# Pooled attention and a rational MoE layer on one core: transfer lengths in the plan by piece size, and the softmax's remainder transposed by VectorE and placed by the weights' transfers

## The chip, the cores and the metric

The kernel runs on one core of one Trainium2 chip. The metric is device time in microseconds (us) of one execution; the result of several runs is their median. Engines are named as in the profile: PE (TensorE's matmuls), PEld (its weight loads), DVE (VectorE), ACT (ScalarE), POOL (GpSimd) and SP (SyncE, which here issues all transfers).

## The reference

```python
# q, k, v: 8 batches x 8 heads x 576 tokens x 64
k_p = k.reshape(B, H, 72, 8, D).mean(axis=3)        # keys and values pooled by 8: 72 a head
v_p = v.reshape(B, H, 72, 8, D).mean(axis=3)
scores = (q @ k_p.T) / sqrt(64)
scores = scores - max(scores)
attn = exp(scores) / (sum(exp(scores)) + 1e-09)
attn_out = attn @ v_p
# then over 4608 tokens x 512:
x = attn_out.transpose(0, 2, 1, 3).reshape(4608, 512)
h = x @ w_in                                        # 512 -> 2048
P = a0 + a1*h + a2*h**2 + a3*h**3
Q = 1 + |b0|*|h| + |b1|*h**2
out = (P / (Q + 1e-6)) @ w_out                      # 2048 -> 512
```

All is f32. The weights `w_in` and `w_out` arrive as 64-bit floats and are decoded in the kernel.

## The kernel before

The 4608 tokens go in 18 blocks of 256 (two tiles of 128 each). For a block, attention gives `x` (512 features by 256 tokens) as a rounded part and a remainder part in fp32r, so that products of three terms keep f32 accuracy. Then eight units follow, each of 256 columns of `w_in`: 24 matmuls into `ph` (`mm1`), a chain of about thirteen elementwise steps on ACT, DVE and POOL (`rational`, `quotient`), and 12 matmuls into `po` (`mm2`). Blocks 0 and 1 do their first four units, then blocks 2 and 3 theirs, while weights still arrive; blocks 4 to 17 follow one by one.

No loop order is issued as written. Every helper (`dve`, `act`, `gp`, `pe`, `dma`) adds an operation to a `Plan` with a cost in us, and `Plan.solve` simulates the engines with these costs: an operation has a due time (from `HEAD`, `SLOW` and `PACE` by the number of its unit, passed back through what it depends on, by `slack` times the cost), may not start in the plan earlier than `early` us ahead of it, and among those that can start the one due first is taken. The order so found on each engine is what is issued; on the chip each engine then keeps that order and waits where an operand is late. A transfer occupies a modelled bus for its bytes over 385 GB/s, then lands 2.2 us later; at most eight are in flight in the plan. `issue` also puts idle matmuls (`filler`, line 265 in the profile) into holes that the plan leaves on PE until 110 us.

Attention for a tile of 128 tokens (`attention`): scores `ps` (PE), maximum and difference into `e` (DVE), exponential (ACT), sum and reciprocal (DVE), normalisation (POOL). `e` holds, for each of four pairs of heads `j`, 2 x 72 = 144 weights a token. They must be transposed (pooled keys onto partitions) to be multiplied with the pooled values in `pv` (`values`). Of the 144, 128 make a full square and 16 are the remainder (`REM`).

- The 128: in blocks 0 to 3 PE transposes them (`pm`), ACT rounds them to `hi` and DVE subtracts to `lo`. From block 4 on DVE transposes 32 x 32 squares in place in `e`, and 16 transfers from `e` to `lo` (`am` in the profile) place the squares; then ACT rounds `lo` to `hi` and DVE subtracts.
- The remainder: in all blocks, ACT and DVE write a rounded and a remaining part, each twice, side by side into `er` (two casts and two subtractions a tile), PE transposes this with two `pr` transposes a tile (fp32r), and ACT copies the result to `ar`. `pv` takes `ar` as one of its four terms, with `vr` as the weights.

`q` is loaded in 32 x 32 squares too from block 4 on (`squares`). `prep_k` and `prep_v_early` or `prep_v` pool keys and values of a batch as soon as a block needs it; for the first two batches the loads go to spare weight tiles (`early`), and PE pools the values (`pvs`, `pvr`).

Of the kernel before, what the change touches and what calls it, by code (L numbers as in the profile page):

```python
# [99 lines left out]
class Plan:  # L100
# [54 lines left out]
    def solve(self):  # L155
# [15 lines left out]
        while done < len(self.ops):  # L171
# [50 lines left out]
            if op.bytes:  # L222
                bus = max(bus, op.end) + op.bytes / 385e3
                op.end = bus + 2.2
                flights = sorted(flights[1:] + [op.end])
# [61 lines left out]
def tile_pooled_attention_then_rational_moe(  # L287
# [20 lines left out]
    P = 128  # L308
# [45 lines left out]

    def dma(kbytes, dst, src, eng="sp", issue=0.48, early=60.0, after=()):
        plan.add(eng, issue, [("dma_start", (dst, src), {})], bytes=kbytes * 1024, early=early,
                 after=after)

# [57 lines left out]
    def scalars():  # L416
        dma(2, ab[:, 0:4], a.partition_broadcast(P), issue=3.7)
        dma(1, ab[:, 4:6], b.partition_broadcast(P))
        for i in range(4):
            small("tensor_scalar", out=abn[:, i:i + 1], in0=ab[:, i:i + 1],  # L420
                                scalar1=-WS ** -i, scalar2=None, op0=ALU.mult)
        act(6).activation(abn[:, 4:6], ab[:, 4:6], AF.Abs)
# [15 lines left out]
    def load_weights(kind, u):  # L438
        name = f"{kind}{u}"
        raw = new("cpool", name, [P, 2 * CW], F32, "r" + name)  # L440
        if kind == "win":
            dma(1024, raw.bitcast(I32).rearrange("p (k x) -> p k x", x=4 * P),
                w_in32[:, u * 4 * P:(u + 1) * 4 * P].rearrange("(k p) x -> p k x", p=P))
        else:
            dma(1024, raw.bitcast(I32).rearrange("p (f x) -> p f x", f=2),
                w_out32[u * 2 * P:(u + 1) * 2 * P, :].rearrange("(f p) x -> p f x", p=P))
        words = raw.bitcast(I32).rearrange("p (n t) -> p n t", t=2)
# [91 lines left out]
    def prep_v(n):  # L539
        rows = v_rows(n)  # L540
        vs_all = new("work1", "vs", [P, 512], F32, f"vs{n}")
        vs = vs_all[:, 0:NJ * D].rearrange("p (j d) -> p j d", d=D)
# [50 lines left out]
    def squares(i):  # L593
# [6 lines left out]
        for r0, r1, n in segs(i * TOK, TOK):  # L600
            s0 = i * TOK + r0 - n * S
            for j in range(NJ):
                for g in range(4):
                    hh, d0 = g // 2, g % 2 * HB
                    dma(3 * (r1 - r0) // 8, qs[g * HB:(g + 1) * HB, j, r0 // HB:r1 // HB, :],
                        q[n, 2 * j + hh, s0:s0 + r1 - r0, d0:d0 + HB].rearrange(
                            "(b s) d -> s b d", s=HB))
        return qs

    def attention(t, am, ar, qs, es):  # L610

# [7 lines left out]
        else:  # L619
# [3 lines left out]
            for r0, r1, n in sg:  # L623
                s0 = t * P + r0 - n * S
                dma(512, qt[r0:r1], q[n, :, s0:s0 + (r1 - r0), :].rearrange("h s d -> s h d"))
            pq = bank(f"pq{t}", [P, NJ, P])
# [4 lines left out]
            act(NJ * P).copy(qT, pq)  # L631
        e = es[:, :, t % 2].rearrange("p j (h s) -> p j h s", s=SP)
        mx = new("work2", "mx", [P, H], F32, f"mx{t}")
        sm = new("work2", "sm", [P, H], F32, f"sm{t}")
        for c in range(2):
# [6 lines left out]
                for jj in range(2) for r0, r1, n in sg], claims=(e, mx, sm))  # L642
# [5 lines left out]
                    [P, 2, 2, SP]), op=ALU.subtract)  # L648
        ef = es[:, :, t % 2]
        act(H * SP).activation(ef, ef, AF.Exp, scale=D ** -0.5)  # L650
# [14 lines left out]
        hi, lo = am  # L665
        if t >= 8:
            squares = ef[:, :, REM:].rearrange("p j (g s) -> p j g s", s=HB)
            dve(NJ * P).transpose(squares, squares)
        else:
            pm = bank(f"pm{t}", [P, NJ, P])  # L670
            pe(109 * NJ, [("transpose", (pm[:, j, :], ef[:, j, REM:], ident), {})
                          for j in range(NJ)], claims=am)
            act(NJ * P).copy(hi[:, :, col], pm)
            dve(NJ * P).tensor_tensor(
                out=lo[:, :, col], in0=pm, in1=hi[:, :, col].bitcast(F32), op=ALU.subtract)
# [5 lines left out]
    def values(i, am, ar):  # L681

        hi, lo = am
# [24 lines left out]
    def attend(i):  # L708

        for _, _, n in segs(i * TOK, TOK):  # L710
            if n not in prepared:
                prepared.add(n)
                prep_k(n)
                (prep_v_early if n < 2 else prep_v)(n)
        am = [new("work1", f"am{s}", [P, NJ, TOK], F32R, f"am{s}_{i}") for s in range(2)]
        ar = new("work1", "ar", [P, 2, TOK], F32R, f"ar{i}")
        qs = squares(i)
        es = new("work1", "e", [P, NJ, 2, 2 * SP], F32, f"e{i}")
        for m in range(2):
            attention(2 * i + m, am, ar, qs, es)  # L720
        if i >= 4:

            hi, lo = am
# [6 lines left out]
            hi, lo = (x.rearrange("p j t -> p (j t)") for x in am)  # L730
            act(NJ * TOK).copy(hi, lo.bitcast(F32))
            dve(NJ * TOK, port=True).tensor_tensor(
                out=lo, in0=lo.bitcast(F32), in1=hi.bitcast(F32), op=ALU.subtract)
        return values(i, am, ar)


    def spill(i, xs):
        kept = []
        for s, x in enumerate(xs):
            d = new("hbm", f"xd{s}_{i}", [P, NJ, TOK], F32, f"xd{s}_{i}")  # L740
            dma(512, d, x.bitcast(F32))
            kept.append(d)
        return kept

    def reload(i, kept):
        xs = [new("work2", f"x{s}", [P, NJ, TOK], F32R, f"xr{s}_{i}") for s in range(2)]
        for x, d in zip(xs, kept):
            dma(512, x.bitcast(F32), d)
        return xs
# [180 lines left out]
```

## Time and profile before

| | |
|---|---|
| median of 3 runs | 962.45 us (959.35 to 963.65) |
| profiled execution | 965.26 us |
| its span | 963.6 us, granted clock 0.993 |
| matmuls on PE | 6261 |
| transfers `am<-e` | 224 of 32 KB |
| moved by DMA | 71.65 MB, 156692 packets |

The span is the time from the first to the last instruction of the profiled execution. A row of a group of instructions gives its line, engine, operation, the tiles written and read, their shapes and the count; then its busy time in us and the mean duration of one in ns; then how long the engine stood idle just ahead of such instructions and what ended that. Since operations are recorded by one helper, nearly all have line 268 (265 for the idle matmuls), so the tiles' names tell them apart. Matmuls are pipelined: what one costs is read from start to start, not from its duration.

### The profile page before, as it was taken

The page shows a single profiled execution, that of the slowest core. Times are in us where ns is not written, and L with a number is a line of the kernel's source. Part 1 is how long each engine was busy: PE and PEld are TensorE (multiplying, and loading weights), DVE is VectorE, ACT ScalarE, POOL GpSimd, SP SyncE. Part 2 cuts the span into 40 slices and gives each one's busy share as a digit, 9 for nine tenths or more (in the row PEclk, how much of TensorE's full clock was granted, in tenths as well). Part 3 has the DMA queues.
Part 4 walks back from the last instruction along what each step waited for, and adds up shares of the span by engine and source line. Part 5 has one row for each costly group of instructions (what it writes and reads, how often), then busy time and mean ns, then how long its engine had stood idle before and what let it go on. Part 6 is the DMA issues. An engine that isn't in the chain of part 4 may idle for free.

```text
span 963.6 us, 17331 instructions
## 1 busy us (share of the span) xinstructions
PE 948.0 (98%) x6261; PEld 860.5 (89%) x6261; DVE 781.6 (81%) x1346; ACT 694.5 (72%) x1180; POOL 509.1 (53%) x445
## 2 busy tenths in 40 slices
PE   8899999999999999999999999999999999999998
PEld 7888899988998999999999899989999899999996
DVE  6787988888888978798888897979787988787664
ACT  4676888958676767676777686776867686767674
POOL 4465556847455645445745374547544654544343
PEclk9989999999999999999999999999999999999999
DMA  9965210154133213122313240214211411102000
GB/s 305 336 233 182 70 57 1 44 138 125 48 70 72 66 20 92 17 51 61 107 18 63 56 122 7 36 41 121 52 28 46 93 41 27 41 1 45 1 22 22
DMA packets 156692, 71.65 MB, mean 74 GB/s; under 512 B 133952, under 2 KB 133952, under 8 KB 156608
## 3 DMA queue, kind: packets, MB, share of 16 engines
q1 hardware_dynamic: 156608, 70.56, 28.0%
q8 instruction: 49, 0.80, 0.3%
q14 instruction: 35, 0.29, 0.1%
HBM read 50.60 MB, written 12.58 MB: 66 GB/s over the span
## 4 chain that ended last, share of the span: by engine, by line
PE 88%; DVE 4%; DMA 2%; SPq 2%; ACT 2%; issue 1%; DVEq 0%
PE po L268 39%; PE ph L268 39%; PE pv L268 4%; PE ps L268 3%; SPq L268 2%; DVE t L268 2%; DMA early<-in_v_dram 2%; DMA q<-in_q_dram 1%; DVE m_wout L268 1%; PE pr L268 1%; PE pk L265 0%; DVE rp L268 0%; ACT t L268 0%; PE pk L268 0%; PE ph L265 0%
## 5 line engine op out<-in xcount | busy, mean ns | idle before, releaser
L268 PEld LDWEIGHTS ph<-x,win 128*128 128x128 f32 x3264 | 482.3, 188 | 61.1 <-ACT t L268 0.8
L268 PE MATMUL ph<-x,win 128*128 128x256 f32 x3264 | 500.8, 281 | 0.6 <-ACT t L268 0.4
L268 PE MATMUL po<-wout,gh 128*128 128x512 f32 x1152 | 358.5, 397 | 0.0
L268 POOL TENSOR_TENSOR w<-w,r 128x512 f32<-128x512 f32 (+1 forms) x145 | 189.7, 1308 | 263.5 <-ACT r L268 252.6
L268 POOL TENSOR_TENSOR gl<-t,gh 128x512 fp32r<-128x512 f32 (+1 forms) x145 | 192.6, 1328 | 100.6 <-ACT gh L268 100.3
L268 PEld LDWEIGHTS po<-wout,gh 128*128 128x128 f32 x1152 | 182.3, 189 | 7.3 <-ACT gh L268 0.2
L268 PE MATMUL po<-wout,gl 128*128 128x512 f32 x576 | 181.6, 396 | 0.0
L268 DVE TENSOR_TENSOR t<-t,ph 128x512 f32<-128x512 f32 (+1 forms) x145 | 97.9, 675 | 61.9 <-ACT t L268 60.1
L268 DVE SCALAR_TENSOR_TENSOR t<-t,abn,rp 128x512 f32<-128x512 f32 (+1 forms) x145 | 106.9, 737 | 48.9 <-ACT rp L268 46.2
L268 ACT ACTIVATE w<-ph 128x512 f32<-128x512 f32 (+1 forms) x145 | 86.1, 594 | 73.6 <-PE ph L268 68.1
L268 ACT ACTIVATE rp<-w,cbias 128x512 f32<-128x512 f32 (+1 forms) x145 | 99.9, 689 | 43.7 <-POOL w L268 41.2
L268 ACT ACTIVATE r<-w,abn 128x512 f32<-128x512 f32 (+1 forms) x145 | 117.9, 813 | 10.7 <-POOL gl L268 4.4
L268 ACT ACTIVATE t<-ph,abn 128x512 f32<-128x512 f32 (+1 forms) x145 | 110.8, 765 | 20.2 <-PE ph L268 14.4
L268 DVE SCALAR_TENSOR_TENSOR t<-t,abn,ph 128x512 f32<-128x512 f32 (+1 forms) x145 | 107.5, 742 | 6.3 <-ACT w L268 1.3
L268 ACT CAST gh<-t 128x512 fp32r<-128x512 f32 (+1 forms) x145 | 88.3, 609 | 23.0 <-DVE t L268 19.9
L268 DVE SCALAR_TENSOR_TENSOR t<-rp,t 128x512 f32<-128x512 f32 (+1 forms) x145 | 99.3, 685 | 4.3
L268 DVE SCALAR_TENSOR_TENSOR rp<-w,rp 128x512 f32<-128x512 f32 (+1 forms) x145 | 99.1, 683 | 0.2
L268 PEld LDWEIGHTS po<-wout,gl 128*128 128x128 f32 x576 | 91.1, 189 | 4.1 <-issue 0.6
L268 ACT ACTIVATE rp<-rp 128x512 f32<-128x512 f32 (+1 forms) x145 | 84.0, 579 | 3.4 <-DVE t L268 0.5
L268 POOL TENSOR_TENSOR e<-e,sm 128x576 f32<-128x576 f32 x36 | 41.5, 1159 | 30.8 <-DVE sm L268 22.3
L268 POOL TENSOR_TENSOR st_v<-st_v 128x512 f32<-128x512 f32 (+1 forms) x36 | 36.5, 1018 | 38.1 <-DMA st_v<-in_v_dram 12.1
L268 PE MATMUL pv<-am,vm 128*128 128x256 f32 (+3 forms) x288 | 47.9, 286 | 0.5 <-DVE kpT L268 0.4
(95 smaller groups left out, 870.3 us busy)
## 6 DMA issues: line engine op xcount, KB each, us to landing
out_dram<-ob SPq DMA_DIRECT2D x17, 512.0 KB, 3.1
rwin<-in_moe_w_in_dram SPq DMA_DIRECT2D x8, 1024.0 KB, 9.0
rwout<-in_moe_w_out_dram SPq DMA_DIRECT2D x8, 1024.0 KB, 10.3
am<-e SPq DMA_DIRECT2D x224, 32.0 KB, 2.0
st_k<-in_k_dram SPq DMA_DIRECT2D x12, 512.0 KB, 4.5
st_v<-in_v_dram SPq DMA_DIRECT2D x12, 512.0 KB, 3.9
q<-in_q_dram SPq DMA_DIRECT2D x144, 32.0 KB, 2.0
st_v<-in_v_dram SPq DMA_DIRECT2D x48, 64.0 KB, 3.8
```

The source lines that it names most:

```text
L268: getattr(engines[op.eng], name)(*map(value, args), **{k: value(v) for k, v in kw.items()})
```

## The change

In the plan: a transfer's bytes are counted as `kbytes * (1 + 312 / run)`, with `run` the length in bytes of its contiguous pieces, over 390 instead of 385 GB/s; the `kbytes` of several transfers are set to their true size in exchange. `HEAD`, `PACE` and one `slack` change, and the `issue` cost of the scalars' load.

In the computation: `e` gets two more columns of squares (`NJ + 2`), and so does `lo`, in place of `er` and `ar`. In blocks 4 to 17 DVE transposes the 2 x 16 remainders of two pairs of heads into each of them, four times side by side; the 16 transfers that place the squares carry these two along (six squares a piece of work instead of four). After the landing ACT rounds the lower 64 partitions of these columns in place, writes the rounded upper 64 to a part of `e`, and DVE subtracts that from the upper 64. In blocks 0 to 3 ACT copies the four-fold remainder (f32), PE transposes it (f32, two a tile), ACT copies the result to `lo` rounded, and DVE subtracts on the upper 64 partitions.

```diff
-                bus = max(bus, op.end) + op.bytes / 385e3
+                bus = max(bus, op.end) + op.bytes / 390e3
...
-    def dma(kbytes, dst, src, eng="sp", issue=0.48, early=60.0, after=()):
-        plan.add(eng, issue, [("dma_start", (dst, src), {})], bytes=kbytes * 1024, early=early,
-                 after=after)
+    def dma(kbytes, dst, src, run=2048, issue=0.48, early=60.0, after=()):
+        plan.add("sp", issue, [("dma_start", (dst, src), {})], early=early, after=after,
+                 bytes=kbytes * 1024 * (1 + 312 / run))
...
-        dma(2, ab[:, 0:4], a.partition_broadcast(P), issue=3.7)
+        dma(2, ab[:, 0:4], a.partition_broadcast(P))
...  # load_weights "wout", spill, reload: run=4096
-        vs_all = new("work1", "vs", [P, 512], F32, f"vs{n}")
+        vs_all = new("work1", "vs", [P, (NJ + 2) * D], F32, f"vs{n}")
...  # squares(i), the q loads of blocks 4 to 17
-                    dma(3 * (r1 - r0) // 8, qs[g * HB:(g + 1) * HB, j, r0 // HB:r1 // HB, :],
+                    dma((r1 - r0) / 8, qs[g * HB:(g + 1) * HB, j, r0 // HB:r1 // HB, :],
...                         run=128
...  # attention, the q loads of blocks 0 to 3
-                dma(512, qt[r0:r1], q[n, :, s0:s0 + (r1 - r0), :].rearrange("h s d -> s h d"))
+                dma(2 * (r1 - r0), qt[r0:r1],
+                    q[n, :, s0:s0 + (r1 - r0), :].rearrange("h s d -> s h d"), run=256)
...
-        er = new("work2", "er", [P, 2, 2, 2, 2, REM], F32R, f"er{t}")
-        rem = ef[:, :, 0:REM].rearrange("p (c m) r -> p c m r", m=2)
-        for c in range(2):
-            esrc = rem[:, c].unsqueeze(1).to_broadcast([P, 2, 2, REM])
-            act(90).copy(er[:, c, 0], esrc)
-            dve(60, port=True).tensor_tensor(
-                out=er[:, c, 1], in0=esrc, in1=er[:, c, 0].bitcast(F32), op=ALU.subtract)
+        main = pairs[:, 0:NJ, REM:]
+        rem = [pairs[:, 2 * c:2 * c + 2, 0:REM].unsqueeze(1).to_broadcast([P, 4, 2, REM])
+               for c in range(2)]
+        four = [pairs[:, NJ + c, REM:].rearrange("p (g m r) -> p g m r", g=4, m=2)
+                for c in range(2)]
         if t >= 8:
+            for c in range(2):
+                dve(P).transpose(four[c], rem[c])
+            squares = main.rearrange("p j (g s) -> p j g s", s=HB)
             dve(NJ * P).transpose(squares, squares)
         else:
...
+            for c in range(2):
+                act(P).copy(four[c], rem[c])
+            pr = bank(f"pr{t}", [P, 2, P])
+            pe(109 * 2, [("transpose", (pr[:, c, :], pairs[:, NJ + c, REM:], ident), {})
+                         for c in range(2)])
+            act(2 * P).copy(lo[:, NJ:, col], pr)
+            dve(2 * P).tensor_tensor(
+                out=lo[P // 2:, NJ:, col], in0=pr[P // 2:],
+                in1=lo[P // 2:, NJ:, col].bitcast(F32), op=ALU.subtract)
-        pr = new("ps", "ps", [P, 2, P], F32R, f"pr{t}")
-        pe(63 * 2, [("transpose", (pr[:, c, :], er[:, c].rearrange("p a g m r -> p (a g m r)"),
-                                   identr), {}) for c in range(2)], claims=(ar,))
-        act(2 * P).copy(ar[:, :, col], pr.bitcast(F32))
...  # values
-                             (pv[:D, jj, r0:r1], vr[n % 2][:, j, :], ar[:, c, r0:r1]),
+                             (pv[:D, jj, r0:r1], vr[n % 2][:, j, :], lo[:, NJ + c, r0:r1]),
...  # attend
-        am = [new("work1", f"am{s}", [P, NJ, TOK], F32R, f"am{s}_{i}") for s in range(2)]
-        ar = new("work1", "ar", [P, 2, TOK], F32R, f"ar{i}")
+        hi, lo = (new("work1", f"am{s}", [P, NJ + 2 * s, TOK], F32R, f"am{s}_{i}")
+                  for s in range(2))
...
-        es = new("work1", "e", [P, NJ, 2, 2 * SP], F32, f"e{i}")
+        es = new("work1", "e", [P, NJ + 2, 2, 2 * SP], F32, f"e{i}")
...
-                    dma(96, lo[g * HB:(g + 1) * HB].rearrange(
+                    dma(48, lo[g * HB:(g + 1) * HB].rearrange(
                         "p j (m a s) -> p j m a s", m=2, s=HB)[:, :, :, a, :].bitcast(F32),
-                        es[a * HB:(a + 1) * HB, :, :, k0:k0 + HB], issue=0.65)
+                        es[a * HB:(a + 1) * HB, :, :, k0:k0 + HB],
+                        run=128, issue=0.65)
...
+            half = slice(P // 2, P)
+            act(2 * TOK).copy(lo[0:P // 2, NJ:], whole[0:P // 2, NJ:])
+            own = es[half, 0:2, :, 0:P]
+            both = [x[half, NJ:].rearrange("p c (m s) -> p c m s", m=2) for x in (lo, whole)]
+            act(2 * TOK).copy(own.bitcast(F32R), both[1])
+            dve(2 * TOK, port=True).tensor_tensor(
+                out=both[0], in0=both[1], in1=own, op=ALU.subtract)
...
-    HEAD, PACE, SLOW, SLOWS = 31.0, 6.3, 5.0, 2 * NA
+    HEAD, PACE, SLOW, SLOWS = 25.0, 6.1, 5.0, 2 * NA
...
-            plan.slack = 1.6
+            plan.slack = 1.4
             xs[i, again] = reload(i, kept.pop(i)) if again else attend(i)
```

More of the change, by code (lines that the diff above doesn't have):

```diff
@@ L445, in load_weights @@
             dma(1024, raw.bitcast(I32).rearrange("p (f x) -> p f x", f=2),
-                w_out32[u * 2 * P:(u + 1) * 2 * P, :].rearrange("(f p) x -> p f x", p=P))
+                w_out32[u * 2 * P:(u + 1) * 2 * P, :].rearrange("(f p) x -> p f x", p=P), run=4096)
         words = raw.bitcast(I32).rearrange("p (n t) -> p n t", t=2)
@@ L604, in squares, with attention @@
                     hh, d0 = g // 2, g % 2 * HB
-                    dma(3 * (r1 - r0) // 8, qs[g * HB:(g + 1) * HB, j, r0 // HB:r1 // HB, :],
+                    dma((r1 - r0) / 8, qs[g * HB:(g + 1) * HB, j, r0 // HB:r1 // HB, :],
                         q[n, 2 * j + hh, s0:s0 + r1 - r0, d0:d0 + HB].rearrange(
-                            "(b s) d -> s b d", s=HB))
+                            "(b s) d -> s b d", s=HB), run=128)
         return qs
-    def attention(t, am, ar, qs, es):
+    def attention(t, hi, lo, qs, es):
         sg = segs(t * P, P)
@@ L631, in attention @@
             act(NJ * P).copy(qT, pq)
-        e = es[:, :, t % 2].rearrange("p j (h s) -> p j h s", s=SP)
+        pairs = es[:, :, t % 2]
+        e = es[:, 0:NJ, t % 2].rearrange("p j (h s) -> p j h s", s=SP)
         mx = new("work2", "mx", [P, H], F32, f"mx{t}")
@@ L648, in attention @@
                     [P, 2, 2, SP]), op=ALU.subtract)
-        ef = es[:, :, t % 2]
+        ef = es[:, 0:NJ, t % 2]
         act(H * SP).activation(ef, ef, AF.Exp, scale=D ** -0.5)
@@ L657, in attention @@
                 [P, NJ, 2, SP]), op=ALU.mult)
-        er = new("work2", "er", [P, 2, 2, 2, 2, REM], F32R, f"er{t}")
-        rem = ef[:, :, 0:REM].rearrange("p (c m) r -> p c m r", m=2)
-        for c in range(2):
-            esrc = rem[:, c].unsqueeze(1).to_broadcast([P, 2, 2, REM])
-            act(90).copy(er[:, c, 0], esrc)
-            dve(60, port=True).tensor_tensor(
-                out=er[:, c, 1], in0=esrc, in1=er[:, c, 0].bitcast(F32), op=ALU.subtract)
-        hi, lo = am
+        main = pairs[:, 0:NJ, REM:]
[3 more added lines that the diff above has]
+                for c in range(2)]
         if t >= 8:
-            squares = ef[:, :, REM:].rearrange("p j (g s) -> p j g s", s=HB)
+            for c in range(2):
+                dve(P).transpose(four[c], rem[c])
+            squares = main.rearrange("p j (g s) -> p j g s", s=HB)
             dve(NJ * P).transpose(squares, squares)
@@ L670, in attention, with values @@
             pm = bank(f"pm{t}", [P, NJ, P])
-            pe(109 * NJ, [("transpose", (pm[:, j, :], ef[:, j, REM:], ident), {})
-                          for j in range(NJ)], claims=am)
+            pe(109 * NJ, [("transpose", (pm[:, j, :], main[:, j], ident), {})
+                          for j in range(NJ)], claims=(hi, lo))
             act(NJ * P).copy(hi[:, :, col], pm)
             dve(NJ * P).tensor_tensor(
-                out=lo[:, :, col], in0=pm, in1=hi[:, :, col].bitcast(F32), op=ALU.subtract)
-        pr = new("ps", "ps", [P, 2, P], F32R, f"pr{t}")
-        pe(63 * 2, [("transpose", (pr[:, c, :], er[:, c].rearrange("p a g m r -> p (a g m r)"),
-                                   identr), {}) for c in range(2)], claims=(ar,))
-        act(2 * P).copy(ar[:, :, col], pr.bitcast(F32))
-    def values(i, am, ar):
-        hi, lo = am
+                out=lo[:, 0:NJ, col], in0=pm, in1=hi[:, :, col].bitcast(F32), op=ALU.subtract)
+            for c in range(2):
[7 more added lines that the diff above has]
+                in1=lo[P // 2:, NJ:, col].bitcast(F32), op=ALU.subtract)
+    def values(i, hi, lo):
         xs = [new("work2", f"x{s}", [P, NJ, TOK], F32R, f"x{s}_{i}") for s in range(2)]
@@ L714, in attend @@
                 (prep_v_early if n < 2 else prep_v)(n)
-        am = [new("work1", f"am{s}", [P, NJ, TOK], F32R, f"am{s}_{i}") for s in range(2)]
-        ar = new("work1", "ar", [P, 2, TOK], F32R, f"ar{i}")
+        hi, lo = (new("work1", f"am{s}", [P, NJ + 2 * s, TOK], F32R, f"am{s}_{i}")
+                  for s in range(2))
         qs = squares(i)
-        es = new("work1", "e", [P, NJ, 2, 2 * SP], F32, f"e{i}")
+        es = new("work1", "e", [P, NJ + 2, 2, 2 * SP], F32, f"e{i}")
         for m in range(2):
-            attention(2 * i + m, am, ar, qs, es)
+            attention(2 * i + m, hi, lo, qs, es)
         if i >= 4:
-            hi, lo = am
             for a in range(4):
@@ L726, in attend @@
                     k0 = REM + g * HB
-                    dma(96, lo[g * HB:(g + 1) * HB].rearrange(
+                    dma(48, lo[g * HB:(g + 1) * HB].rearrange(
                         "p j (m a s) -> p j m a s", m=2, s=HB)[:, :, :, a, :].bitcast(F32),
-                        es[a * HB:(a + 1) * HB, :, :, k0:k0 + HB], issue=0.65)
-            hi, lo = (x.rearrange("p j t -> p (j t)") for x in am)
-            act(NJ * TOK).copy(hi, lo.bitcast(F32))
+                        es[a * HB:(a + 1) * HB, :, :, k0:k0 + HB],
+                        run=128, issue=0.65)
+            whole = lo.bitcast(F32)
+            act(NJ * TOK).copy(hi, whole[:, 0:NJ])
             dve(NJ * TOK, port=True).tensor_tensor(
-                out=lo, in0=lo.bitcast(F32), in1=hi.bitcast(F32), op=ALU.subtract)
-        return values(i, am, ar)
+                out=lo[:, 0:NJ], in0=whole[:, 0:NJ], in1=hi.bitcast(F32), op=ALU.subtract)
+            half = slice(P // 2, P)
[5 more added lines that the diff above has]
+                out=both[0], in0=both[1], in1=own, op=ALU.subtract)
+        return values(i, hi, lo)
     def spill(i, xs):
@@ L740, in spill @@
             d = new("hbm", f"xd{s}_{i}", [P, NJ, TOK], F32, f"xd{s}_{i}")
-            dma(512, d, x.bitcast(F32))
+            dma(512, d, x.bitcast(F32), run=4096)
             kept.append(d)
@@ L747, in reload @@
         for x, d in zip(xs, kept):
-            dma(512, x.bitcast(F32), d)
+            dma(512, x.bitcast(F32), d, run=4096)
         return xs
```

## The prediction

> **What bounds the kernel now.** I read the busy lines of the page first, then the busy time by stretches, then what PE waited for.
>
> ```profile
> PE 948.0 (98%) x6261; PEld 860.5 (89%) x6261; DVE 781.6 (81%) x1346; ACT 694.5 (72%) x1180; POOL 509.1 (53%) x445
> 24.10:60.00 35.90, 33.19 (x238) 31.71 (x237) 25.23 (x45) 24.75 (x43) 16.54 (x10) 0.90 1.00 334
> 40.00:50.00 10.00, 8.15 (x43) 7.24 (x43) 5.36 (x10) 3.98 (x9) 2.16 (x2) 0.79 1.06 334
> 50.00:60.00 10.00, 10.00 (x71) 9.75 (x70) 7.69 (x10) 7.74 (x13) 5.24 (x4) 0.86 0.94 320
> 60.00:80.00 20.00, 18.07 (x119) 17.42 (x118) 14.40 (x24) 12.77 (x20) 10.92 (x7) 0.83 0.38 138
> 500.00:600.00 100.00, 100.00 (x673) 90.86 (x672) 85.26 (x148) 73.11 (x126) 52.89 (x45) 1.00 0.26 60
> ```
>
> A row by stretches gives the length, then PE, PEld, DVE, ACT and POOL busy, the granted clock, the DMA share and GB/s. There are two regimes. From about 106 us on, PE has no holes (100.00 of 100, clock 1.00); the other engines and the DMA have room, and only fewer PE microseconds shorten the time. Before that the head is bound elsewhere: DMA share 1.00 at 334 GB/s until 60 us, and the granted clock falls to 0.79 to 0.86 between 40 and 80. What PE waited for from 106 us to the end are five waits that sum to 2.0 us, of which this is the longest:
>
> ```profile
> PE pk L268 <- DVE ks L268: 0.6, 1, 0.6
> ```
>
> **The change, part by part.** The profiled execution took 965.26 us, its span 963.6; the median of the runs is 962.45, 2.8 lower. I make the sum against 965.26 and carry the difference over to the median.
>
> *Transposes of the remainder leave PE, blocks 4 to 17.* Each of these 14 blocks has four `pr` transposes (two tiles, two each). PE's timeline with and without them, at the same mix of neighbours:
>
> ```profile
> 543.85 0.63 PE L268 MATMUL ph<-x,win 128*128 128x256 f32 x4
> 544.32 0.46 PE L268 MATMUL pr<-identr,er 128*128 128x128 f32 x4
> 544.62 0.70 PE L268 MATMUL po<-wout,gh 128*128 128x512 f32 x2
> 545.15 0.63 PE L268 MATMUL ph<-x,win 128*128 128x256 f32 x4
> ...
> 504.43 0.64 PE L268 MATMUL ph<-x,win 128*128 128x256 f32 x4
> 504.90 0.62 PE L268 MATMUL po<-wout,gh 128*128 128x512 f32 x2
> 505.36 0.63 PE L268 MATMUL ph<-x,win 128*128 128x256 f32 x4
> L268 PE MATMUL pr<-identr,er 128*128 128x128 f32 x72 | 9.2, 242 | 1.5 <-DVE t L268 0.9 <-ACT ar L268 0.5 <-DVE er L268 0.2
> ```
>
> From `ph` to `ph` it is 1.30 us with them and 0.93 without: 0.37 us a block, 14 times, 5.2 us. Ends: start to start alone, 0.30 x 14 = 4.2; the group's busy time, 9.2 x 56/72 = 7.2. I take 5.2, since it includes what the neighbours lose. It is all on the path, since PE is never idle there.
>
> *Blocks 0 to 3* keep two transposes per tile, now f32 instead of fp32r. The nearest f32 transposes are `pm`:
>
> ```profile
> 95.11 0.60 PE L268 MATMUL pm<-identr,e 128*128 128x128 f32 x4
> 95.47 0.70 PE L268 MATMUL po<-wout,gl 128*128 128x512 f32 x2
> ```
>
> Four in 0.36 us, 0.09 each, as the `pr` above (0.37/4). I take 0; the ends are -0.3 and +0.3 us for 16. The DVE subtraction now follows `pr` instead of going ahead of it; the chain has as many steps as before.
>
> *ACT, DVE and POOL, blocks 4 to 17.*
>
> ```profile
> L268 ACT CAST er<-e 128x64 fp32r<-128x64 f32 x72 | 13.8, 240 | 9.4 <-POOL e L268 8.9
> L268 ACT CAST ar<-pr 128x256 fp32r<-128x256 f32 x36 | 11.9, 376 | 2.4 <-PE pr L268 2.3
> L268 DVE TENSOR_TENSOR er<-e,er 128x64 fp32r<-128x64 f32 x72 | 21.1, 336 | 0.5 <-ACT er L268 0.5
> L268 ACT CAST x<-pv 128x512 fp32r<-128x512 f32 x36 | 21.1, 586 | 19.5 <-PE pv L268 19.4
> L268 DVE TENSOR_TENSOR x<-pv,x 128x512 fp32r<-128x512 f32 x36 | 24.5, 686 | 15.0 <-ACT x L268 14.9
> L268 DVE STREAM_TRANSPOSE e<-e 128x512 f32<-128x512 f32 x28 | 18.6, 689 | 0.0
> L268 ACT CAST am<-am 128x1024 fp32r<-128x1024 f32 x14 | 14.6, 1042 | 5.8 <-DMA q<-in_q_dram 4.7 <-DMA am<-e 1.1
> ```
>
> ACT loses four casts `er` and two `ar` a block (0.96 + 0.75 = 1.71 us) and gains two 512-element copies on 64 partitions (0.59 each by `x`, 1.18): 0.5 us less. DVE loses four subtractions (0.29 each, 21.1/72: 1.17) and gains four 128-element transposes and one 512-element subtraction (0.69). A transpose of 512 takes 0.69; I estimate 0.30 for 128, between a quarter of that and the 0.34 of the 64-element row, so 1.89 in all: 0.7 us more a block. DVE is at 85% in these stretches, so 43 becomes 44 of 50 us; its cover is the 7 us a block in which it is idle. POOL does nothing new. Cost 0 on the path, end +0.
>
> *The transfers that place the weights* stay 16 a block and 128 bytes a piece, but grow from 32 to 48 KB each.
>
> ```profile
> am<-e SPq DMA_DIRECT2D x224, 32.0 KB, 2.0
> q<-in_q_dram SPq DMA_DIRECT2D x144, 32.0 KB, 2.0
> q<-in_q_dram SPq DMA_DIRECT2D x48, 8.0 KB, 1.6
> L268 SPq DMA_DIRECT2D am<-e x224: 585/609/1797, 225.1 to 877.9; - x112
> ```
>
> From 8 to 32 KB landing grows by 0.4 us, so 16 KB more cost about 0.3 us. Issue takes SP 0.61 us; between no growth and growth with the pieces (0.91) I take the lower, since nothing shows growth, and keep 4.9 us a block as the end. Queued behind them on SP are the next block's `q` loads and the output's store. The Trainium skill ("DMA: Bandwidth & Descriptors", "Why small descriptors are slow (HBM only)") says that transfers inside SBUF do not pay for small pieces as those from HBM do; the two 32 KB rows above, one from SBUF and one from HBM, both land in 2.0 us, so here the latency hides any such difference.
>
> *The new tail of the chain, and who waits for it.* After the last landing stood one ACT cast and one DVE subtraction; now two ACT copies (1.18) and a DVE subtraction (0.69) follow before `pv` has its third operand, and two transposes (0.6) stand ahead of the transfers: with the landing 1.18 + 0.69 + 0.6 + 0.3 = 2.8 us. On PE, `pv` has all later `ph` and `po` behind it. The tightest of the 14 blocks and the next tightest (the last row is for the sentence behind):
>
> ```profile
> 492.75 1.22 DVE L268 TENSOR_TENSOR am<-am,am 128x1024 fp32r<-128x1024 f32 x1
> 496.70 0.39 PE L268 MATMUL pv<-am,vm 128*128 128x256 f32 x2
> ...
> 291.19 1.22 DVE L268 TENSOR_TENSOR am<-am,am 128x1024 fp32r<-128x1024 f32 x1
> 298.51 0.47 PE L268 MATMUL pv<-am,vm 128*128 128x256 f32 x2 [0.44 <-DVE kpT L268]
> ...
> 500.00 1.14 PE L268 MATMUL ps<-kpT,qT 128*128 128x144 f32 x8
> ```
>
> 2.7 us lie between in the first pair, 6.1 in the second, more in the other twelve. So 0 to 0.1 us there, and 0 elsewhere. `e` serves as scratch in the tail and is held some 3 us longer; the next block writes it after its first `ps`, at 500.00, 6.0 us behind the end of the subtraction in the tightest block, which covers that.
>
> *The plan.* `issue` for the scalars' load falls from 3.7 to 0.48 us, which moves what SP does next that much forward in the plan alone. A full 1 MB transfer was planned at 2.72 us (1 MiB over 385 GB/s); now 3.10 in 2 KB runs. At the 334 GB/s of the stretch from 24 to 60 us it takes 3.14. So the plan comes to know that loads land later. What this is worth lies in the head:
>
> ```profile
> 41.91 1.10 PE L268 MATMUL pvs<-early,identr 128*128 128x256 f32 x4
> 44.87 2.82 PE L268 MATMUL pvr<-early,fourfold 32*128 32x128 f32 x16 [1.85 <-DMA early<-in_v_dram]
> 69.31 4.76 PE L265 MATMUL pk<-identr 128*128 128x128 f32 x23 [1.93 <-DVE t L268]
> 74.17 3.70 PE L265 MATMUL ph<-identr 128*128 128x256 f32 x20
> ```
>
> PE was sent to `pvr` before its transfer had landed, stood 1.9 us, and lost clock: (1 - 0.79) x 10 + (1 - 0.86) x 10 = 3.5 us. That hole costs 5.4. A plan with true landing times puts ready `ph` work there. I take half, 2.7, since an order that is filled in one place can open in another; ends -5.4 (gone) and +5.4 (a second such hole). The second hole, 69 to 78, waits on DVE and is filled by 8.5 us of idle matmuls; I leave it, with 1.9 + 8.5 = 10.4 us as the far end. The Trainium skill ("TensorE: Matmul & The Clock Gate", Part 1) puts the loss of clock behind an idle window of about 3.4 us; here 1.9 us of waiting, after thin work, was enough, so I price by the rows.
>
> *HEAD, PACE, slack.* `HEAD` 31 to 25 and `PACE` 6.3 to 6.1 bring due times forward, attention's slack 1.6 to 1.4 puts its chain later against the weights; the head's idle matmuls may end 6 us sooner. After 106 us there are only 2.0 us of waits to win, so 0; in the head it is part of the -5.4 to +5.4.
>
> Sum: 965.26 - 5.2 - 2.7 = 957.4 against the profiled execution, 954.6 against the median.
>
> **The rivals.**
> - Only the transposes count; the head's holes move but stay: 962.45 - 5.2 = 957.3. For it: DMA share 1.00 until 60 us, whatever the order.
> - Both holes of the head go: 962.45 - 5.2 - 5.4 - 10.4 = 941.5 at most, some 946 if half of the second one goes. Against it: that one is DVE's backlog, and DVE gets no less to do.
> - The new order opens a second hole like that at 44.87 (fillers end sooner, weights go ahead of `v`): 962.45 - 5.2 + 5.4 = 962.7, no change. By the page of the Trainium skill named above a hole below 3.4 us would cost its wait alone, 1.9 instead of 5.4, so 959.2; the 0.79 of the clock row here speaks against it.
> - Slower: the longer tail reaches `pv` in blocks 4 to 17. If smaller slack in the plan brings the margins of 6 us and more down to nothing, each block waits up to 2.8 us, 39 in all; at half of that 954.6 + 20 = 974. It decides from 0.9 us a block on ((967.3 - 954.6)/14). For it: the margin of 2.7 us in one block. Against it: the other margins.
>
> **How the numbers follow.** Forecast 0.40 (its own range 950 to 957.6), only the transposes 0.20, both holes 0.15, a new hole 0.15, late `pv` 0.10. Within 0.5% means 957.6 to 967.3, about what a measurement of this kernel tells from no change. Faster: 0.40 + 0.11 of the second case, which sits on the bound, + 0.15 = 0.66. Same: 0.09 + 0.12 + 0.02 = 0.23. Slower: 0.03 + 0.08 = 0.11. The range, 945 to 963, leaves out late `pv` and the best of both holes.
>
> **What would show it.** In the profile after: `pr` 16 instead of 72 on PE and 0.93 us between neighbours in blocks 4 to 17; `am` transfers of 48 KB landing in about 2.3 us; DVE's share in the stretches from 200 on up one to two points with PE still at 100; no wait of PE `pvr` on a load and a clock above 0.9 from 40 to 60. Wrong if PE waits for `pv`'s operands after 200 us, if a 128-element transpose takes far over 0.30, or if the head, up to the point where PE runs without holes, is later than before.

## The result, and the profile after

The changed kernel takes 955.11 us (median of 5 runs, 954.91 to 955.53) against 960.92 of the kernel before beside it (5 runs, 959.35 to 963.65): ratio 0.9936, 95% interval 0.9917 to 0.9955. It is faster by 0.64%, forecast at 954.6. Together with the runs beside the experiments it is 955.0 (11 runs, 953.38 to 955.76) against 962.3 (the 91 runs of the kernel before beside the experiments, 957.88 to 970.07), 7.3 us less. The two profiled executions, 965.26 and 955.0, lie 10.3 us apart; part of that is chance in the kernel before, as e3 shows.

The page's busy line and clock line, then rows by stretches (length, PE, PEld, DVE, ACT and POOL busy, granted clock, DMA share, GB/s):

```profile
PE 938.6 (98%) x6203; PEld 851.1 (89%) x6203; DVE 801.7 (84%) x1352; ACT 693.7 (73%) x1124; POOL 509.9 (53%) x445
...
PEclk9989999999999999999999999999999999999999
```

```profile
40.00:50.00 10.00, 10.00 (x86) 9.96 (x85) 9.37 (x12) 10.00 (x16) 8.27 (x5) 1.00 1.07 329
50.00:60.00 10.00, 8.53 (x45) 7.23 (x44) 9.74 (x16) 5.34 (x9) 5.01 (x3) 0.89 1.03 377
60.00:80.00 20.00, 18.57 (x108) 15.37 (x108) 14.74 (x23) 15.22 (x25) 11.71 (x9) 0.88 0.36 129
...
500.00:600.00 100.00, 99.90 (x666) 90.38 (x665) 90.42 (x153) 73.15 (x118) 54.80 (x45) 1.00 0.31 65
```

PE is busy 9.4 us less, and is still nearly without holes once the head is over (0.1 us in this stretch, 2.3 in the 824 from 106 to 930). DVE is busy 20 us more: at 90 of 100 in this stretch where it had 85. The stretch from 40 to 50, at clock 0.79 before, is full now. Where the profile before lost clock from 40 to 60 and once more from 60 to 80 (0.83), this one loses it from 50 to 80 alone.

The groups that took the place of `er`, `ar` and 56 of the 72 `pr` (busy us, mean ns of one, idle ahead of it):

```profile
L268 PE MATMUL pr<-identr,e 128*128 128x128 f32 x16 | 3.1, 277 | 0.0
L268 DVE STREAM_TRANSPOSE e<-e 128x128 f32<-128x128 f32 x56 | 14.2, 280 | 3.8 <-POOL e L268 3.7
L268 DVE TENSOR_TENSOR am<-am,e 64x512 fp32r<-64x512 f32 x14 | 9.8, 698 | 0.4
L268 ACT CAST e<-am 64x512 fp32r<-64x512 f32 x14 | 8.7, 618 | 0.3
am<-e SPq DMA_DIRECT2D x224, 48.0 KB, 2.2
L268 SPq DMA_DIRECT2D am<-e x224: 585/618/1821, 217.6 to 870.6; - x112
```

What PE waited for in the head and after it, the longest rows:

```profile
PE pk L268 <- DVE ks L268: 2.0, 2, 1.6
PE idle L268 <- DVE identr L909: 1.7, 1, 1.7
PE pvr L268 <- DVE t L268: 1.5, 1, 1.5
PE ps L268 <- ACT qT L268: 1.1, 1, 1.1
PE pm L265 <- DVE am L268: 1.1, 1, 1.1
PE ph L265 <- DVE e L268: 0.9, 1, 0.9
```

No row of the whole list names a transfer, and none names `pv`. The chain's new tail in the tightest of the 14 blocks, between DVE's last subtraction and `pv`:

```profile
288.50 0.69 DVE L268 TENSOR_TENSOR am<-am,e 64x512 fp32r<-64x512 f32 x1
...
291.14 0.40 PE L268 MATMUL pv<-am,vm 128*128 128x256 f32 x2
```

It ends 1.95 us ahead of it (288.50 + 0.69 to 291.14); in the second profile of the same kernel (e5) the same block has 1.63.

### The profile page after: what moved, and what is told of

It reads as the page before. It is cut to its first block, busy times and chain, and to the rows that moved or that the text cites. A ratio compares the mean times of both kernels' runs of the same rounds, so it can differ in the third digit from the quotient of the medians.

```text
span 953.3 us, 17151 instructions
## 1 busy us (share of the span) xinstructions
PE 938.6 (98%) x6203; PEld 851.1 (89%) x6203; DVE 801.7 (84%) x1352; ACT 693.7 (73%) x1124; POOL 509.9 (53%) x445
## 4 chain that ended last, share of the span: by engine, by line
PE 81%; DVE 6%; ACT 4%; SPq 3%; issue 2%; POOL 2%; DMA 1%; DVEq 0%; POOLq 0%; ACTq 0%
PE ph L268 36%; PE po L268 35%; PE ps L268 4%; PE pv L268 3%; SPq L268 3%; DVE t L268 2%; ACT rp L268 1%; PE idle L265 1%; PE pvs L268 1%; DMA am<-e 1%; POOL w L268 1%; DVE m_win L268 1%; POOL gl L268 1%; DVE rp L268 1%; DVE e L268 1%
## 5 line engine op out<-in xcount | busy, mean ns | idle before, releaser
L268 ACT ACTIVATE e<-e 128x576 f32<-128x576 f32 x36 | 24.3, 681 | 40.8 <-DVE e L268 40.8
```

The costliest lines, as they stand in the source:

```text
L268: getattr(engines[op.eng], name)(*map(value, args), **{k: value(v) for k, v in kw.items()})
```

## The experiments

Times are medians. Comparisons of less than 1% are made at equal granted clock too, for the reason that e3 gives; times at a given clock are means over the runs with that mean clock.

**e3: the kernel before, again.** No edit.

> The kernel before, unchanged, for a second profile. The runs so far lie between 959.35 and 965.26, those of after within 0.6 us. Theory: the spread of before arises in the head, where PE waits for a load at about 45 us and loses clock: the start of block 4's pv lies some us earlier than the 251.3 of the first profile, and from there to the end it takes the same 712 us within 0.5. Rival: the spread is spread over the whole run, in proportion.

Measured: 962.53 (959.37 to 967.54, 12 runs). Its profile is one of the better executions, 960.81 us with span 959.1. The same stretches as in the prediction's first fence:

```profile
40.00:50.00 10.00, 8.70 (x49) 7.90 (x50) 5.57 (x8) 3.74 (x7) 3.30 (x2) 0.84 1.07 339
50.00:60.00 10.00, 10.00 (x82) 9.81 (x81) 8.90 (x11) 9.30 (x15) 5.72 (x5) 0.99 1.03 359
60.00:80.00 20.00, 18.10 (x131) 16.02 (x129) 16.11 (x32) 14.84 (x24) 11.09 (x8) 1.00 0.40 143
```

The same program, the same two waits on the `early` load (2.0 and 1.0 us here, 0.9 and 1.9 in the first profile), and yet a clock of 0.99 and 1.00 where it was 0.86 and 0.83. In narrower stretches the clock stands at 0.50: for 6.8 us, twice, in the first profile, and for 3.4 us, once, in this one. One such row of each:

```profile
45.90:52.70 6.80, 6.80 (x31) 6.49 (x31) 1.34 (x3) 3.16 (x6) 2.39 (x1) 0.50 0.91 320
46.70:50.10 3.40, 3.40 (x18) 3.40 (x18) 0.69 (x1) 1.77 (x3) 2.14 (x1) 0.50 1.02 393
```

That is 6.8 and 1.7 us of PE's time lost (half of 13.6 and of 3.4). Where the two executions part is seen at the first `pv` rows of block 4 (instructions' shortest/mean/longest in ns, then the stretch in us), the first profile and then this one:

```profile
L268 PE MATMUL pv<-am,vm x24: 271/275/317, 251.3 to 254.4; 128*128 128x128 f32 x24
```

```profile
L268 PE MATMUL pv<-am,vm x24: 271/275/318, 246.3 to 249.4; 128*128 128x128 f32 x24
```

5.0 us lie between them there, for 5.1 us of lost clock; from there to the end of the span it is 712.3 us (963.6 - 251.3) and 712.8 (959.1 - 246.3). So between these two executions of one kernel the difference arises in the head, in the clock that its thin stretches lose in one execution and keep in another. The 91 runs of the kernel before, by their mean granted clock (80 of them; the other 11 lie between these columns or below 0.989):

| granted clock | 1.000 | 0.998 | 0.996 | 0.995 | 0.993 | 0.991 | 0.989 |
|---|---|---|---|---|---|---|---|
| mean, us | 958.6 | 960.2 | 962.2 | 963.6 | 965.4 | 966.8 | 969.0 |
| runs | 7 | 23 | 14 | 8 | 16 | 9 | 3 |

About 1 us for each 0.001 of mean clock, which is what 0.001 of a span of 960 us comes to. The runs are from three chips, whose means at 0.998 are 960.0, 960.2 and 960.3. The Trainium skill ("TensorE: Matmul & The Clock Gate", Part 1) says that the window in which the gate counts busy cycles runs freely, so that the moment of a change of clock varies from run to run; that fits this table, and the stretches of 3.4 and 6.8 us at 0.50; no run here shows what the gate counts. Against this, the changed kernel's 11 runs split into 955.1 at 0.996 (6) and 954.4 at 0.998 (5). At equal clock the change is worth 7.1 us (0.996) and 5.8 us (0.998). The changed kernel pays 0.7 us for the same 0.002 that cost the kernel before 2.0, so this comparison too depends on the clock at which it is made.

**e1: the new computation alone, with the plan of before** (the lengths of before, its `issue` of 3.7, HEAD, PACE and slack).

```diff
-                bus = max(bus, op.end) + op.bytes / 390e3
+                bus = max(bus, op.end) + op.bytes / 385e3
...
-                 bytes=kbytes * 1024 * (1 + 312 / run))
+                 bytes=kbytes * 1024)
...
-    HEAD, PACE, SLOW, SLOWS = 25.0, 6.1, 5.0, 2 * NA
+    HEAD, PACE, SLOW, SLOWS = 31.0, 6.3, 5.0, 2 * NA
...
-            plan.slack = 1.4
+            plan.slack = 1.6
```

> The new computation (remainder transposed by VectorE from block 4 on, carried by the weights' transfers) under the plan of before: 385 GB/s without the term for the pieces, HEAD 31, PACE 6.3, slack 1.6, issue 3.7. Theory: taking the pr transposes off PE is worth 4 to 5 us by itself: about 956.0 (0.995 of before), and PE's waits after 106 us stay under 4 us. Rival: the new order of the plan carries the gain and the transposes give nothing net, since DVE and the longer tail take it back: 960 to 962.

**e2: the old computation with the new plan**, the same edits the other way, in the kernel before.

> The computation of before (pr on PE, er, ar) under the new plan: lengths by pieces, 390 GB/s, HEAD 25, PACE 6.1, slack 1.4, issue 0.48. Theory: 1 to 2 us faster than before, from the head alone: 959 to 960. Rival (the plan carries the gain): 955 to 956. A second rival (the new due times suit only the new computation): 962 to 966.

Measured: e1 955.57 us (954.05 to 960.08, 9 runs), ratio 0.9933, interval 0.9906 to 0.9960: the whole gain without the plan. e2 963.87 (962.01 to 966.11, 12 runs), ratio 1.0020, 0.9997 to 1.0042: nothing, or 1 to 2 us lost. At equal clock (0.996) e1 takes 954.6 and the changed kernel 955.1; e2 takes 964.2 at 0.993 and 962.8 at 0.995, about 1 us less than the kernel before there (965.4 and 963.6), but none of its runs lies above 0.995. So the plan's new numbers bring nothing that shows in the time, with either computation. The stretches that lose most in e1, and in e2, and in e2 the longest wait there:

```profile
60.00:80.00 20.00, 15.89 (x92) 13.50 (x91) 16.35 (x32) 11.15 (x18) 9.27 (x7) 0.83 0.70 231
```

```profile
80.00:106.00 26.00, 20.89 (x94) 15.18 (x95) 21.43 (x39) 16.79 (x30) 13.27 (x9) 0.80 0.35 110
94.81 0.73 PE L268 MATMUL po<-wout,gh 128*128 128x512 f32 x2 [2.14 <-ACT gh L268]
```

In e1 the stretch 40 to 60 is full at clock 1.00, with no wait on the load, although its plan has the old, too short times of the loads; it loses from 60 to 80 instead. In e2 that stretch has clock 1.00, and most of the loss is at 80 to 106. Each order has its thin place in the head, somewhere else in each. e1 loses clock once more in the middle: 3.4 us at half clock from 537 on, behind a wait of 1.8 us on DVE. Lost clock is not confined to the head.

**e4: two f32 transposes a tile back on PE in blocks 4 to 17.** Their results go to a bank that nobody reads.

```diff
                 dve(P).transpose(four[c], rem[c])
+            pr = bank(f"pr{t}", [P, 2, P])
+            pe(109 * 2, [("transpose", (pr[:, c, :], main[:, c], ident), {}) for c in range(2)])
             squares = main.rearrange("p j (g s) -> p j g s", s=HB)
             dve(NJ * P).transpose(squares, squares)
```

> After, with two f32 transposes a tile on PE put back in blocks 4 to 17 (of the weights' first two squares, into a bank that nothing reads): extra work, so that only PE's price of them is measured. Theory: PE has no holes there, so all 56 show, 0.09 each: 955.1 + 5.0 = 960.1 (4.2 to 5.2 more). Rival: PE has slack there that hides them: 955 to 956.

Measured: 962.77 us (957.34 to 964.86, 12 runs), at equal clock 962.3 (0.998) and 964.2 (0.996), so 8 to 9 us more than the changed kernel, and more than the 5.0 expected. It does not price the transposes alone: PE reads `e` here, which DVE transposes in place, so DVE has to wait for PE. But in the profiled execution, the fastest of the twelve (957.34, clock 1.00), that happens once:

```profile
DVE e L268 <- PE pr L268: 0.7, 1, 0.7
```

So this wait is not shown to be the cause of the excess, which stays open. e6 does without it.

**e6: the same transposes, of the identity**, which wait for nothing and which nobody waits for; and **e5: the changed kernel again**, beside it.

```diff
+            pr = bank(f"pr{t}", [P, 2, P])
+            pe(109 * 2, [("transpose", (pr[:, c, :], ident, ident), {}) for c in range(2)])
```

> After, with two f32 transposes of the identity a tile on PE in blocks 4 to 17, which wait for nothing and which nothing reads: PE's price of 56 transposes by itself, without the wait that the earlier version of this put between PE and VectorE's transposes. Compared at equal granted clock with after. Theory: 0.09 each, 5.0 more (4.2 to 5.8). Rival: the whole 7 us by which after is lower at equal clock is PE's price: 7 or more.

> After, unchanged, among runs of before on one chip. In the runs so far the time goes with the granted clock of the whole run: before took 958 at 1.000, 960 at 0.998, 962 at 0.996, 965 at 0.993, 967 at 0.991. Theory: that is the clock PE loses in the head, another amount in each execution; after follows the same line about 7 us lower: 955 at 0.996, 951 to 952 at 1.000 if that comes, 958 at 0.993. Rival: after is steadier than before and stays within 1 us.

Measured: e5 954.5 us (953.38 to 955.76, 6 runs), ratio 0.9903, 0.9873 to 0.9933: 955.1 at 0.996 as the theory had it, but 954.2 at 0.998, where its line gives 953, and a spread of 2.4 us, so neither the theory nor the rival holds. e6 960.76 (958.19 to 962.2, 12 runs), ratio 0.9969, 0.9948 to 0.9990. At equal clock that is 6.2 us (0.998) and 6.5 us (0.996) above the changed kernel, for 56 transposes on PE and the order that the planner makes with them: between the theory's 4.2 to 5.8 and the rival's 7. In PE's timeline of e6 (start, duration):

```profile
402.94 0.63 PE L268 MATMUL ph<-x,win 128*128 128x256 f32 x4
403.40 0.62 PE L268 MATMUL po<-wout,gh 128*128 128x512 f32 x2
403.87 0.60 PE L268 MATMUL pr<-identr 128*128 128x128 f32 x4
404.22 0.72 PE L268 MATMUL ph<-x,win 128*128 128x256 f32 x4
404.77 0.63 PE L268 MATMUL po<-wout,gl 128*128 128x512 f32 x2
```

Four take 0.35 us from start to start (403.87 to 404.22), and the `ph` behind them 0.55 to the next start where it takes 0.46 without (402.94 to 403.40): 0.43 to 0.44 us a block, 6.1 in 14. That agrees with the time of the whole: once the head is over, more work on PE shows as time.

**e7: blocks 0 to 3 as before**, with the fp32r remainder `er` from ACT and DVE ahead of PE (in the buffer of `ks`, since its own is gone).

```diff
-            for c in range(2):
-                act(P).copy(four[c], rem[c])
-            pr = bank(f"pr{t}", [P, 2, P])
...
+            er = new("work1", "ks", [P, 2, 2, 2, 2, REM], F32R, f"er{t}")
+            for c in range(2):
+                esrc = old[:, c].unsqueeze(1).to_broadcast([P, 2, 2, REM])
+                act(90).copy(er[:, c, 0], esrc)
+                dve(60, port=True).tensor_tensor(
+                    out=er[:, c, 1], in0=esrc, in1=er[:, c, 0].bitcast(F32), op=ALU.subtract)
...
+            act(2 * P).copy(lo[:, NJ:, col], pr.bitcast(F32))
```

> After, with the remainder in blocks 0 to 3 formed as before (two casts and two subtractions a tile into a tile er, which shares its place with ks, two fp32r transposes on PE, one copy). Compared at equal clock with after. Theory: of the 7 us at equal clock 2 to 3 come from the head, by the new form in blocks 0 to 3: 957 to 958 at 0.996. Rival: the form in the head is worth nothing (955 to 955.5 at 0.996), and blocks 4 to 17 carry all.

Measured: 957.01 us (955.28 to 958.18, 7 runs), ratio 0.9931, 0.9902 to 0.9960; at equal clock 956.2 (0.998) and 957.5 (0.996), so 1.8 to 2.4 us more than the changed kernel, from three runs at each clock (at 0.998 two lie near 955.3 and one at 957.8). Its thin place lies late in the head:

```profile
80.00:106.00 26.00, 21.78 (x137) 18.55 (x136) 20.45 (x45) 17.35 (x32) 10.96 (x8) 0.87 0.45 144
```

Whether these 2 us are the old form's own work, its buffers, or the other order that the planner makes around it, this run doesn't tell: the order of the head differs from the first blocks on, and the table further down shows that its profile loses them behind block 4's start.

**e8: DVE's new 128-element transposes done twice**, 56 more of them.

```diff
-                dve(P).transpose(four[c], rem[c])
+                for _ in range(2):
+                    dve(P).transpose(four[c], rem[c])
```

> After, with the 56 transposes of the remainder on VectorE in blocks 4 to 17 done twice (the second repeats the first): 14 us more on VectorE in all, 1.0 a block, its share from 88 to 90% in the middle. Theory: still off the path, since pv's operands are ready 2 us and more ahead: 955 to 957 at 0.996. Rival: VectorE is at its limit, and PE waits for most of it: 962 to 969.

Measured: 955.7 us (953.92 to 958.37, 6 runs), ratio 0.9916, 0.9884 to 0.9947; at clock 0.998 955.1 (three runs, 953.9 to 955.8), 0.7 us more than the changed kernel. The group, and six blocks in the middle, first of e8 and then, for the same stretch, of the changed kernel:

```profile
L268 DVE STREAM_TRANSPOSE e<-e 128x128 f32<-128x128 f32 x112 | 28.7, 290 | 6.0 <-POOL e L268 4.3
200.00:500.00 300.00, 297.86 (x1960) 269.73 (x1959) 264.02 (x474) 218.69 (x354) 164.43 (x136) 1.00 0.33 71
```

```profile
200.00:500.00 300.00, 299.81 (x1983) 272.43 (x1982) 263.61 (x459) 218.66 (x356) 160.85 (x136) 1.00 0.33 73
```

The transposes take 14.5 us more (28.7 by 14.2), and the time grows by 0.7 us, as the theory had it. But DVE as a whole is busy only 6.6 us more (808.3 by 801.7), and in the 300 us shown only 0.4, since other operations of DVE came out shorter. PE has 2.1 us of holes in the 300 instead of 0.2.

**e9 and e10: the plan's two halves undone one at a time**, in the changed kernel: e9 the due times (HEAD 31, PACE 6.3, slack 1.6, with the new lengths), e10 the lengths and `issue` (with the new due times). The edits are the two halves of e1's.

> After with HEAD 31, PACE 6.3 and slack 1.6 as before; the lengths by pieces stay. The plan as a whole gave nothing at equal clock (after 955.1 at 0.996, the new computation under the old plan 954.6), but after's runs lie within 2.4 us (953.4 to 955.8), those under the old plan within 6 (954.1 to 960.1). Theory: the lengths by pieces are what steadies the head, so this one stays within 2.5 us and at 954 to 956.5. Rival: the due times do it, and this one spreads over 5 us and more, up to 960.

> After with the lengths as before (385 GB/s, no term for the pieces, issue 3.7); HEAD 25, PACE 6.1, slack 1.4 stay. Theory (the lengths steady the head): spreads over 5 us and more, 954 to 961. Rival (the due times): within 2.5 us, 954 to 956.5.

Measured: e9 964.68 us (961.93 to 966.24, 12 runs), ratio 1.0017, 0.9992 to 1.0043, so some 9.7 us above the changed kernel; e10 969.2 (965.77 to 970.79, 12 runs), ratio 1.0062, 1.0040 to 1.0085, some 14 above. Neither expectation came, nor either rival: the spreads are 4.3 and 5.0 us, the times far above both. Their clocks (0.989 to 0.995) and those of the changed kernel (0.996 and 0.998) do not overlap, so part of the 9.7 and 14 is lost clock. What PE waited for longest and the stretch that lost most, of e9:

```profile
PE pk L268 <- DVE ks L268: 2.9, 3, 1.6
PE pr L265 <- DVE am L268: 1.8, 1, 1.8
PE po L268 <- DVE ob L268: 1.7, 2, 1.3
60.00:80.00 20.00, 16.95 (x111) 15.12 (x110) 15.37 (x32) 12.93 (x23) 10.75 (x7) 0.83 0.77 255
```

and of e10 the longest wait and its stretch:

```profile
PE pvs L268 <- DMA early<-in_v_dram: 3.8, 1, 3.8
40.00:50.00 10.00, 7.12 (x33) 6.59 (x33) 6.49 (x11) 5.14 (x9) 4.00 (x2) 0.66 1.08 346
```

Both halves together 955.0, neither (e1) 955.6, one alone 964.7 or 969.2. With the old lengths and the new due times PE is sent ahead of the load again, waits 3.8 us and falls to 0.66; with the true lengths it isn't, in either set of due times, but the old due times then give a string of smaller waits on DVE. With both old (e1) there is no wait on the load either. Neither half has a worth of its own.

**e11: the new path from block 3 on**, to take 20 more transposes off PE (1.8 us by the expectation; four of them are of the 16 `pr` left).

```diff
-        if t >= 8:
+        if t >= 6:
...
-        if i >= 4:
+        if i >= 3:
```

> After with the path of blocks 4 to 17 (q and weights in 32x32 squares, transposed by VectorE and placed by transfers) from block 3 on. It takes two tiles' four pq, four pm and two pr off PE, 20 transposes of 0.09: 1.8 us less, if PE is the bound by the time of block 3 (107 to 128 us). Theory: 953.0 at after's clock, 1.5 to 2 below after. Rival: the head up to there is bound by VectorE and SP, and the longer chain makes pv of block 3 late: 955 to 960.

Measured: 967.69 us (964.48 to 972.04, 12 runs), ratio 1.0044, 1.0020 to 1.0069, 12.7 above the changed kernel, and above the rival's range too. The longest wait and its stretch:

```profile
PE pv L268 <- DVE x L268: 3.6, 1, 3.6
80.00:106.00 26.00, 20.78 (x123) 18.09 (x122) 22.96 (x43) 16.02 (x24) 11.16 (x8) 0.88 0.38 125
```

Block 3 belongs to the head, where PE waits on DVE; the longer chain made a `pv` wait 3.6 us, as the rival had it, and the order turned out worse by far more than the 20 transposes are worth. No variant here is clearly ahead of the changed kernel.

## Why the prediction was right, and where it was not

The time and the sign came out as forecast (954.6; measured 955.0 to 955.1). The sum behind them was right in its main term; the plan's term of -2.7 is not borne out, and some 2 us that the sum does not have came instead. That the total fits to half a microsecond is luck.

*Transposes off PE, -5.2 (4.2 to 7.2): right.* `pr` went from 72 to 16, and the neighbours now start 0.94 us apart in PE's timeline of the changed kernel, the 0.93 forecast:

```profile
535.39 0.64 PE L268 MATMUL ph<-x,win 128*128 128x256 f32 x4
535.87 0.63 PE L268 MATMUL po<-wout,gh 128*128 128x512 f32 x2
536.33 0.64 PE L268 MATMUL ph<-x,win 128*128 128x256 f32 x4
```

e6 shows the step that the argument rests on, that PE's time here is the kernel's, with transposes a little dearer than the removed ones (0.43 us a block for f32 of e6 by 0.37 for fp32r).

The traces also show where the gain lies. In each of them the 385th of the 1728 `po` matmuls, with which `mm2` of block 4 begins if the units keep their order, starts at the time below (us). Behind it PE has the same matmuls left in every one, but for 52 `pr` (of 13 blocks; 48 in e4) where they are on PE, and four `ph`, about 0.5 us, that before, e3 and e1 have already done. The lost clock is half the time at 0.50.

| | before | e3 | e2 | e1 | after | e5 | e7 | e6 | e4 |
|---|---|---|---|---|---|---|---|---|---|
| `pr` left | 52 | 52 | 52 | 0 | 0 | 0 | 0 | 52 | 48 |
| start of the 385th `po` | 275.2 | 270.2 | 275.6 | 267.5 | 268.9 | 268.1 | 268.8 | 268.7 | 268.4 |
| clock lost ahead of it | 6.8 | 1.7 | 6.8 | 3.4 | 3.4 | 1.7 | 3.4 | 1.7 | 0 |
| from it to the end | 688.4 | 688.9 | 686.8 | 685.4 | 684.3 | 684.2 | 686.7 | 691.8 | 687.3 |

From there on the changed kernel takes 4.1 to 4.7 us less, 4.6 to 5.2 with the four `ph`; 13 blocks at 0.37 are 4.8. But e2, which has the 52 transposes, is only 2.5 us above the changed kernel, e4 3.1 and e6 7.5, and e7, which does not have them, 2.4. So the term is right, and the order that the planner makes moves this stretch too, by some 2 us.

*Blocks 0 to 3, 0 (±0.3): not settled.* I priced 16 transposes on PE and took the chain as equally long. I left out that on DVE, which ends about half of PE's waiting in the head (5.0 of 9.6 us before), four subtractions a block (0.29 us each) go and two (0.43 each, on the upper 64 partitions) come, and that the part ahead of `pr` gets shorter. e7 puts the old form at +1.8 to +2.4 us. But in its profile block 4's first `po` starts at 268.8, as early as in the changed kernel, and the 2.4 us come behind it, where PE waits 5.2 us instead of 2.6. So they are not shown to be the form's price in blocks 0 to 3. With the lost clock taken off, the head is 2.0 to 3.0 us shorter in after and e5 (265.5 and 266.4) than in before and e3 (268.4 and 268.5); e1 and e7 have that too (264.1 and 265.4), e2 has not (268.8). It comes with the new computation, by which part of it stays open.

*ACT and DVE, 0: right as far as the runs go, and the durations too.* The 128-element transpose takes 0.28 us (estimate 0.30), the copies 0.62 (0.59), the subtraction 0.70 (0.69). By the groups in the form of before and after, DVE's new work is 24.0 us for 16.4 in blocks 4 to 17, 0.54 a block instead of 0.7. From 106 to 930 DVE's share rose by 2.3 points (686.5 to 705.1 us); the 5 points from 500 to 600 are in good part the pooling of keys (`st_k`), of which 8.1 us instead of 4.9 fall into that stretch. Nearly as much as the new work, 7.0 us over the run, comes from a small operation that the change does not touch, which went from 338 to 530 ns:

```profile
L268 DVE TENSOR_SCALAR sm<-sm 128x8 f32<-128x8 f32 x36 | 18.9, 530 | 1.0
```

It takes 238 in e1, 540 in e2, 291 in e8 and 584 in e7, and in second profiles of one program 393 (e3) and 550 (e5). So it goes with the order more than with the computation; what it collides with stays open. e8 puts 14.5 us more of transposes on DVE without PE waiting for most of it, but as DVE's total grew by 6.6 us only, it doesn't show that the cover holds for twice the work.

*Transfers and issue: right.* 48 KB land in 2.2 us (2.3 forecast), issue takes SP 0.618 instead of 0.609, and nothing waits for it; the end of 0.91 did not come.

*The longer tail: right.* The margin of 1.95 us in the tightest block (1.63 in e5) is what is left; no `pv` waits for its operands after 200 us. The late `pv`, 974, did not come.

*The plan, -2.7 (ends ±5.4): wrong.* What I had named did happen: no wait of `pvr` on a load, the stretch 40 to 50 full at clock 1.00. But another place opened 10 us later. PE's timeline after:

```profile
53.40 1.89 PE L268 MATMUL pvs<-early,identr 128*128 128x256 f32 x8
56.76 2.83 PE L268 MATMUL pvr<-early,fourfold 32*128 32x128 f32 x16 [1.47 <-DVE t L268]
64.83 0.98 PE L265 MATMUL ph<-identr 128*128 128x256 f32 x6 [0.67 <-ACT qT L268]
```

`pvr` now waits 1.5 us on DVE, and the clock is 0.89 and 0.88 from 50 to 80: (1 - 0.89) x 10 + (1 - 0.88) x 20 = 3.5 us, as much as I had counted for the hole that went ((1 - 0.79) x 10 + (1 - 0.86) x 10). The first profile before lost another 0.17 x 20 = 3.4 us from 60 to 80, which after doesn't; but e3 lost 1.7 in all and e5 as much, so which execution is profiled decides that. The step of the sum that failed is "puts ready `ph` work there": it did, and a wait on DVE took the place of the wait on the load. e1 and e2 give the term as nothing in the time, and the due times, which I took as 0, are worth 10 us in one combination (e9), the lengths 14 in another (e10), and both nothing in e1. A reading of the rows could not have told that: the planner's order moves the time by 10 us and more, and the rows of before show one order only. I had the rival "only the transposes", 957.3, at 0.20; as a mechanism it is nearer to what ran than my forecast, short by about 2 us whose cause stays open.

*The level.* I carried 965.26 over to the median with -2.8. That this was the state of the head's clock, and that the kernel before moves by 10 us with it (958.6 at 1.000, 969.0 at 0.989), showed only in e3. The forecast difference, 7.9, stands against 5.8 to 7.1 at equal clock and 7.3 over all runs: 4 to 5 in blocks 4 to 17 and 2 to 3 ahead of them fill that, and the plan by itself (e2) has none of it in the time.

*The rule on the clock gate* (the Trainium skill, "TensorE: Matmul & The Clock Gate", Part 1). For a hole below 3.4 us the rule would charge the wait alone. In the runs here waits of 2.0 and 1.0 us came with 0.84 in one stretch (e3), 0.9 and 1.9 with 0.79 and then 0.86 (before), and 3.8 us with 0.66 (e10). After the same wait of `pvr` on DVE, 1.5 us, the changed kernel lost 3.4 us of clock in one profile and 1.7 in the other (e5). So thin work with short waits costs clock here, and by how much varies between executions of one program.

## What to carry to other kernels

Find the stretch in which one engine has no holes, and price a change there by that engine's timeline from start to start, neighbours included: 0.93 us was forecast that way, and 0.94 came. Where a planner writes the order, a changed number in one place reorders a start-up that waits on everything in turn; don't book a gain for one hole that goes, run the plan's numbers apart from the computation and in combination. Before reading a difference under 1%, run the kernel before again and compare at equal granted clock.

## What the runs showed of the hardware

- The granted clock of one program differs between executions (0.987 to 1.000 over 91 runs), and with it the time, about 1 us for each 0.001 in the kernel before; in the profiles of before (both) and after, the clock is 1.00 from 106 to 930 us and 0.94, 0.98 and 0.97 ahead of that. Where it is lost, it stands at 0.50, for 3.4 or 6.8 us at a time in the profiles of before (both), after and e5.
- Four f32 transposes of 128 between other matmuls cost 0.43 us, 0.35 from start to start and 0.08 on the matmul behind them; four fp32r ones cost 0.37 in all. Each is read at one place of a timeline.
- A transfer inside SBUF in 128-byte pieces takes 0.2 us longer to land with 48 KB than with 32 KB, and the queue's issue 0.01 us longer.
- A `TENSOR_SCALAR` on 128x8 takes 238 to 584 ns on average, by the program that it stands in, and up to 55 ns more or less in two executions of one program.
